# A one-column activation ahead of ScalarE's queue, and two weight splits placed behind exponentials, in an attention and feed-forward kernel

## The chip, the core and the metric

The kernel runs on one core of a Trainium2 chip. A core has TensorE (PE, matrix products into PSUM banks), VectorE (DVE), ScalarE (ACT), GpSimd (POOL) and SyncE (SP), which issues most of the transfers. The metric is the device time of one execution in microseconds (us), the median of several runs.

## What is computed

Four batches of eight heads with 576 positions of 64 values pass through attention with random features, then through two feed-forward blocks:

```python
q_p, k_p = phi(q * s), phi(k * s)   # phi(x) = exp(proj - sq - max) / sqrt(m), proj = x @ omega.T
num, den = q_p @ (k_p.T @ v), q_p @ sum(k_p)
x = num / den                        # 2304 tokens x 512
x = ((x @ w_a) * (x @ w_b)) @ w_out  # 1536 hidden
out = relu(x @ w_in2) ** 2 @ w_out2  # 2048 hidden
```

The weights of the feed-forward blocks arrive as 64-bit numbers, whose two 32-bit words the kernel itself turns into a pair of fp32r values (a high and a low part).

## The kernel before

**The stages.** First a prologue (`prologue`, L233) makes an identity matrix, transposes omega on TensorE into PSUM (L245), and copies it in three forms on ScalarE (OMS L247, OMZ L250, twice, and OM L251). Then lanes of attention work run, written as generators. `k_steps` (L407) handles a pair of k heads: it loads k and v (L310, L410), transposes k in four products (`t1_main`, L324; the product is L330, the copy from PSUM is S, L333), projects onto omega (`phi_wide`, L278: product L285, minimum over features on VectorE L289, exponentials on ScalarE L291, one for each head and slab), and multiplies the features with v (L423). `kt_steps` does the same for the last 64 positions of two pairs (the "tail": transpose L273, copy T L275, `phi_wide`, product L396). `q_steps` transposes and projects q, and forms the quotient that becomes a stretch of `x_all`. The lanes of the first batch stand at the beginning (`start_lanes`, L805): the first k pair alone, then q pairs and k pairs by turns. After them come passes over blocks of 256 tokens and weight columns `f` (`a_units`, products L610 and L635), with the rest of the attention lanes woven in, and at the end the second feed-forward block.

**The weights.** `load` (L125) fetches one or two 512 KB pieces into a `raw` buffer, of which there are two. `split` (L142) turns them into the high and low parts: on ScalarE L151, L152 and L163, on VectorE L155, L159, L164, L168 and L172. `load_split` (L184) issues the loads at once, and puts the split on a list with a count of steps; `step()` counts down and `split_next` runs the split when the count is zero, at the latest when the weights are needed. `get_w(f)` asks for w_a and w_b of column block f with a count of 3, `get_wo(n)` for w_out's rows. The first of them are asked for between the steps of the first lanes: `get_w(0)` after the lanes' second step, `get_wo(0)` after the eighteenth.

**What sets the order.** The code's order is only the first word. A planner that knows the dependencies, but estimates durations and transfers, puts the instructions of each engine into a fixed order when the program is built; what it takes to be ready first goes first, and the engine's queue then waits for its instructions one after the other. PSUM banks are handed out in turn by `at_bank` (L228), eight of them, so that the first q pair's transposes take the bank of omega's transpose. Loads on SP stand in one queue: omega, k, v, w_a, w_b, q, the next k, w_out and so on.

Of the kernel before, what the change touches and what calls it, by code (L numbers as in the profile page):

```python
# [8 lines left out]
F32 = mybir.dt.float32  # L9
# [4 lines left out]
ACTF = mybir.ActivationFunctionType  # L14
# [21 lines left out]
def f32(ap):  # L36
    return ap.bitcast(F32)


def i32(ap):  # L40
    return ap.bitcast(I32)
# [3 lines left out]
def kernel(  # L45
# [13 lines left out]
    nc = tc.nc  # L59
# [18 lines left out]
    wpool = ctx.enter_context(tc.tile_pool(name="wpool", bufs=FA))  # L78
# [46 lines left out]
    def load(*parts):  # L125


        raw = top["raw"].tile([128, 2, 512, 2], I32, tag="raw", name="raw")
        for x, (w, f, rows) in enumerate(parts):
            t = raw[:, x]  # L130
            if rows:
                nc.sync.dma_start(
                    out=t.rearrange("p f w -> p (f w)"), in_=w[f * 128:(f + 1) * 128, :]
                )
            else:
                nc.sync.dma_start(
                    out=t.rearrange("p (k f) w -> p k (f w)", k=KC),
                    in_=w[:, f * 256:(f + 1) * 256].rearrange("(k p) f -> p k f", p=128),
                )
        return raw[:, 0:len(parts)]  # L140

    def split(raw, t):  # L142

        n = raw.shape[1]
        up = raw[:, :, :, 1]
        u = raw[:, :, :, 0]
        a = top["cut"].tile([128, 2, 512], F32, tag="a", name="a")[:, 0:n]
        p = top["cut"].tile([128, 2, 512], F32, tag="p", name="p")[:, 0:n]  # L150
        nc.scalar.activation(out=a, in_=f32(up), func=ACTF.Copy, scale=WORD_SCALE)  # L151
        nc.scalar.activation(  # L152
            out=u, in_=raw.bitcast(U16)[:, :, :, 1], func=ACTF.Copy, scale=2.0 ** 7,
        )
        nc.vector.tensor_scalar(  # L155
            out=i32(p), in0=i32(a), scalar1=3, scalar2=0x7FFFF000,
            op0=ALU.logical_shift_left, op1=ALU.bitwise_and,
        )
        nc.vector.scalar_tensor_tensor(  # L159
            out=i32(p), in0=i32(a), scalar=-0x80000000, in1=i32(p),  # L160
            op0=ALU.bitwise_and, op1=ALU.bitwise_or,
        )
        nc.scalar.copy(out=t[:, :, 0, :], in_=p)  # L163
        nc.vector.scalar_tensor_tensor(  # L164
            out=u.bitcast(U32), in0=up.bitcast(U32), scalar=23, in1=u.bitcast(U32),
            op0=ALU.logical_shift_left, op1=ALU.bitwise_or,
        )
        nc.vector.tensor_scalar(  # L168
            out=i32(a), in0=i32(p), scalar1=-0x00800000, scalar2=None,
            op0=ALU.bitwise_and,  # L170
        )
        nc.vector.scalar_tensor_tensor(  # L172
            out=t[:, :, 1, :], in0=u.bitcast(U32), scalar=2.0 ** -43, in1=a,
            op0=ALU.mult, op1=ALU.mult,
        )
# [4 lines left out]
    def split_next():  # L180
        _, _, fn = waiting.pop(0)
        fn()

    def load_split(key, parts, t, steps, then=None):  # L184
        while len(waiting) > 1:
            split_next()
        raw = load(*parts)

        def fn():
            split(raw, t)  # L190
            if then:
                then()

        waiting.append([steps, key, fn])
# [11 lines left out]
    def get_pair(key, steps, pool, tag, *parts):  # L206
        t = pool.tile([128, 2, 2, 512], F32R, tag=tag, name=tag)
        load_split(key, parts, t, steps)
        return t[:, 0], t[:, 1]
# [4 lines left out]
    ap2 = actx.enter_context(tc.tile_pool(name="ap2", bufs=2))  # L214
# [11 lines left out]
    state = {"at": [0, 1, 2, 3, 4, 5, 6, 7], "n": 0}  # L226

    def at_bank(shape, name):  # L228
        i = state["at"][state["n"] % len(state["at"])]
        state["n"] += 1  # L230
        return bank(i, shape, name)

    def prologue():  # L233
        make_identity(nc, ident)
        nc.sync.dma_start(out=om[:, 0, :], in_=omega)
        nc.sync.dma_start(out=om[:, 1, :], in_=omega)


        nc.vector.memset(V, 1.0)
        nc.vector.memset(VT, 1.0)  # L240
        nc.vector.memset(VT[64:128, :, :, 0, :], 0.0)
        nc.vector.memset(VT[0:64, :, :, 1, :], 0.0)
        nc.vector.memset(OMZ, 0.0)
        ps = at_bank([128, M], "ps_om")
        nc.tensor.transpose(ps, om.rearrange("p a d -> p (a d)"), ident)  # L245

        nc.scalar.mul(out=OMS, in_=ps, mul=-SCALE)  # L247
        for x in range(2):
            r = slice(64 * x, 64 * x + 64)
            nc.scalar.mul(out=OMZ[r, x, :], in_=ps[r], mul=-SCALE)  # L250
        nc.scalar.copy(out=OM[:, 0, :], in_=OMS)  # L251
        nc.vector.tensor_tensor(out=OM[:, 1, :], in0=OMS, in1=f32(OM[:, 0, :]), op=ALU.subtract)
# [25 lines left out]
    def phi_wide(rows, dst):  # L278


        n = 2 * len(rows)
        nm = ap2.tile([128, n], F32, tag="nm", name="nm", bufs=4)
        ps = at_bank([128, n, M], "ps_p")
        for x, s in enumerate(rows):
            nc.tensor.matmul(  # L285
                ps[:, 2 * x:2 * x + 2].rearrange("p h m -> p (h m)"), lhsT=s,
                rhs=OMZ.rearrange("p h m -> p (h m)"), start=True, stop=True,
            )
        nc.vector.tensor_reduce(out=nm, in_=ps, axis=AXX, op=ALU.min)  # L289
        for x in range(n):  # L290
            nc.scalar.activation(  # L291
                out=dst[:, x, :], in_=ps[:, x, :], func=ACTF.Exp, scale=-1.0,
                bias=nm[:, x:x + 1],
            )

    class Side:
# [41 lines left out]
        def proj(self, slabs, dst):  # L338

            oo = [i * 128 for i in slabs]
            if self.wide:
                phi_wide([self.s[:, o:o + 128] for o in oo], dst)
                yield
                return
            for n, o in enumerate(oo):
                nm = ap2.tile([128, 2], F32, tag="nm", name="nm", bufs=4)
                ps = at_bank([128, 2, 2, M], "ps_p")
                for x in range(2):  # L350
                    nc.tensor.matmul(  # L351
                        ps[:, x].rearrange("p a m -> p (a m)"), lhsT=self.s[:, x, o:o + 128],
                        rhs=OM.rearrange("p a m -> p (a m)"), start=True, stop=True,
                    )
                c = ap2.tile([128, 2, M], F32, tag="c", name="c", bufs=2)
                nc.scalar.copy(out=c, in_=ps[:, :, 1, :])  # L356
                for x in range(2):
                    nc.vector.tensor_tensor_reduce(  # L358
                        out=c[:, x, :], in0=ps[:, x, 0, :], in1=c[:, x, :], scale=1.0,
                        scalar=3.0e38, op0=ALU.add, op1=ALU.min, accum_out=nm[:, x:x + 1],  # L360
                    )
                for x in range(2):
                    nc.scalar.activation(
                        out=dst[:, 2 * n + x, :], in_=c[:, x, :], func=ACTF.Exp, scale=-1.0,
                        bias=nm[:, x:x + 1],
                    )
                yield
# [5 lines left out]
    def kt_steps(b, g):  # L373
# [13 lines left out]
        yield  # L387
        kp = ap2.tile([128, 2, M], F32, tag="qp", name="kpt", bufs=2)
        phi_wide([st], kp)
        yield  # L390

# [123 lines left out]
    def qt_steps(b, g):  # L515
# [4 lines left out]
        yield  # L520
        qp = ap2.tile([128, 2, M], F32, tag="qp", name="qp", bufs=2)
        phi_wide([st], qp)
        yield
        ps = at_bank([128, 2, 128], "ps_qt")
# [70 lines left out]
    wa, wb, wo = {}, {}, {}  # L595
# [205 lines left out]


    prologue()

    def start_lanes():  # L805
# [23 lines left out]


    def get_w(f):
        wa[f], wb[f] = get_pair(("a", f), 3, wpool, "w", (w_a, f, False), (w_b, f, False))

    wo_order = [(pi, f) for pi, x in enumerate(PASSES) for f in range(x[1], x[2])]
    wo_made = set()
# [37 lines left out]
    def get_first():  # L873
        for f in range(W_FIRST):
            get_w(f)
            yield
            yield
            get_wo(f)
            yield
        for f in range(W_FIRST, 3):  # L880
            get_wo(f)
            yield
# [112 lines left out]
```

## Time and profile before

| | us |
|---|---|
| median of 3 runs | 1050.73 |
| lowest and highest of them | 1049.35, 1052.2 |
| the profiled execution, its own time | 1052.61 |
| span of the profiled execution | 1050.8 |

The span runs from the first to the last instruction that the profile holds; the execution's own time has 1.81 us around it. All times below are counted from the span's start. In rows of the timeline the columns are the start, the time from the first to the last of the instructions merged in the row, the engine, the line, the operation, the tile written and those read, the shape and the count; in brackets stands how long the engine had waited and what ended the wait.

### The profile page before, as it was taken

Reading aid. Unit: us, or ns where it says so; the run is one execution under the profiler, and the core shown is the slowest. Engines: PE = TensorE matmul, PEld = TensorE weight load, DVE = VectorE, ACT = ScalarE, POOL = GpSimd, SP = SyncE. Lnnn points to the kernel's source line nnn. Section 1 sums busy time; section 2 is a strip of 40 time slices with the busy share of each in tenths; the row PEclk is TensorE's granted clock in tenths of the full one; section 3 lists DMA queues with packets and bytes.
Section 4 is the critical chain, followed back from the end, with each engine's and each line's share of the span. In section 5 each row is a group of like instructions: output and inputs, shape, how many; then the busy total and the mean of one; then the engine's idle time right before and its main releaser. Section 6 shows DMA issues by size and latency. Waiting matters only on the chain.

```text
span 1050.8 us, 14948 instructions
## 1 busy us (share of the span) xinstructions
PE 1024.0 (97%) x5641; PEld 873.6 (83%) x5641; DVE 526.8 (50%) x1274; ACT 471.2 (45%) x1079; POOL 28.9 (3%) x54
## 2 busy tenths in 40 slices
PE   4899999999999999999999999999999999999998
PEld 3789989999988877788888888788788888888887
DVE  4788885665654445444337987722222322322222
ACT  4887757554455443333326665522322322322232
POOL 3100101000000000000000000000000000000000
PEclk9999999999999999999999999999999999999999
DMA  6846864663432211312227664300200200100010
GB/s 166 242 148 205 267 233 120 210 209 95 142 105 80 63 46 56 95 62 70 66 87 264 230 220 174 107 1 0 81 1 1 71 1 1 51 1 1 0 41 21
DMA packets 83144, 105.90 MB, mean 101 GB/s; under 512 B 26240, under 2 KB 65152, under 8 KB 83072
## 3 DMA queue, kind: packets, MB, share of 16 engines
q1 hardware_dynamic: 81536, 103.37, 30.7%
q0 software_dynamic: 1536, 1.58, 0.5%
q8 instruction: 45, 0.74, 0.3%
q14 instruction: 27, 0.22, 0.1%
HBM read 87.62 MB, written 17.30 MB: 100 GB/s over the span
## 4 chain that ended last, share of the span: by engine, by line
PE 88%; DVE 4%; DMA 3%; ACT 3%; issue 1%; SPq 1%; ACTq 0%; DVEq 0%
PE abw L610 19%; PE o L764 19%; PE ph L777 18%; PE y L635 12%; PE ab L610 7%; PE ps_n L481 3%; PE ps_p L285 2%; PE ps_kv L423 2%; PE ps_p L351 2%; PE ps_qt L474 1%; DMA raw<-in_moe_w_out_dram 1%; PE ps_t L330 1%; DMA qn<-in_q_dram 1%; DVE p L159 1%; PE ps_x L492 1%
## 5 line engine op out<-in xcount | busy, mean ns | idle before, releaser
L635 PE MATMUL y<-gs,wo 128*128 128x256 f32 (+1 forms) x864 | 177.2, 345 | 0.0
L764 PE MATMUL o<-w,ss 128*128 128x512 f32 x702 | 170.9, 390 | 1.4 <-ACT ss L786 1.4
L777 PE MATMUL ph<-yx,w 128*128 128x512 f32 (+1 forms) x780 | 169.8, 368 | 0.0
L777 PEld LDWEIGHTS ph<-yx,w 128*128 128x128 f32 x780 | 137.4, 188 | 25.3
L785 DVE TENSOR_TENSOR r<-r 128x512 f32<-128x512 f32 (+1 forms) x80 | 51.1, 639 | 209.8 <-ACT r L784 209.8
L764 PEld LDWEIGHTS o<-w,ss 128*128 128x128 f32 x702 | 130.5, 188 | 29.7 <-ACT ss L786 2.2
L635 PEld LDWEIGHTS y<-gs,wo 128*128 128x128 f32 x864 | 136.6, 190 | 15.2
L610 PE MATMUL abw<-x_all,w 128*128 128x512 f32 x576 | 146.6, 398 | 0.0
L784 ACT ACTIVATE r<-ph 128x512 f32<-128x512 f32 (+1 forms) x80 | 44.5, 556 | 208.4 <-PE ph L777 208.2
L610 PE MATMUL ab<-x_all,w 128*128 128x256 f32 x864 | 132.9, 295 | 0.3 <-DVE x_all L549 0.2
L610 PEld LDWEIGHTS abw<-x_all,w 128*128 128x128 f32 x576 | 105.5, 189 | 19.2
L610 PEld LDWEIGHTS ab<-x_all,w 128*128 128x128 f32 x864 | 115.0, 193 | 1.5 <-DVE x_all L549 0.5
L787 DVE TENSOR_TENSOR ss<-r,ss 128x512 fp32r<-128x512 f32 (+1 forms) x80 | 51.1, 639 | 46.6 <-ACT ss L786 40.0
L610 PE MATMUL abw<-x_mid,w 128*128 128x512 f32 x288 | 73.1, 400 | 0.0
L786 ACT CAST ss<-r 128x512 fp32r<-128x512 f32 (+1 forms) x80 | 46.2, 577 | 51.5 <-DVE r L785 51.5
L610 PEld LDWEIGHTS abw<-x_mid,w 128*128 128x128 f32 x288 | 52.1, 189 | 9.8
L358 DVE CUSTOM_DVE_ANT_0 c<-ps_p,c 128x128 f32<-128x128 f32 x152 | 37.8, 287 | 32.5 <-ACT c L356 32.0
L701 ACT CAST gs<-a_s 128x256 fp32r<-128x256 f32 (+1 forms) x96 | 40.6, 433 | 28.3 <-DVE a_s L700 28.1
L164 DVE SCALAR_TENSOR_TENSOR raw<-raw 128x1024 uint32<-128x1024 uint32 (+1 forms) x40 | 42.5, 1062 | 13.4 <-ACT raw L152 13.3
L152 ACT ACTIVATE raw<-raw 128x1024 int32<-128x1024 uint16 (+1 forms) x40 | 40.8, 1020 | 11.4 <-DMA raw<-in_moe_w_out_dram 9.3
L702 DVE TENSOR_TENSOR gs<-a_s,gs 128x256 fp32r<-128x256 f32 (+1 forms) x96 | 42.8, 454 | 5.3 <-ACT gs L701 4.2
L151 ACT ACTIVATE a<-raw 128x1024 f32<-128x1024 f32 (+1 forms) x40 | 40.6, 1014 | 10.9 <-DMA raw<-in_moe_w_out_dram 5.6
(109 smaller groups left out, 1212.9 us busy)
## 6 DMA issues: line engine op xcount, KB each, us to landing
wo<-wo_d SPq DMA_DIRECT2D x60, 512.0 KB, 3.5
raw<-in_moe_w_out_dram SPq DMA_DIRECT2D x28, 512.0 KB, 4.8
raw<-in_moe_w_in_dram SPq DMA_DIRECT2D x16, 512.0 KB, 3.9
raw<-in_moe_w_a_dram SPq DMA_DIRECT2D x12, 512.0 KB, 4.8
raw<-in_moe_w_b_dram SPq DMA_DIRECT2D x12, 512.0 KB, 6.1
wo_d<-wo SPq DMA_DIRECT2D x12, 512.0 KB, 3.4
kn<-in_k_dram SPq DMA_DIRECT2D x16, 256.0 KB, 3.5
V<-in_v_dram SPq DMA_DIRECT2D x16, 256.0 KB, 3.4
```

The source lines that it names most:

```text
L151: nc.scalar.activation(out=a, in_=f32(up), func=ACTF.Copy, scale=WORD_SCALE)
L152: nc.scalar.activation(out=u, in_=raw.bitcast(U16)[:, :, :, 1], func=ACTF.Copy, scale=2.0 ** 7,)
L164: nc.vector.scalar_tensor_tensor(out=u.bitcast(U32), in0=up.bitcast(U32), scalar=23, in1=u.bitcast(U32), op0=ALU.logical_shift_left, op1=A ...
L610: nc.tensor.matmul(ps, lhsT=wv[:, s_, kc, :], rhs=x[..., kc, m_, :], start=(kc == 0 and (s_, m_) == TERMS[0]), stop=(kc == KC - 1 and (s_, ...
L635: nc.tensor.matmul(y_part(pi, f, c), lhsT=wo[pi, f][:, s_, c * 128:(c + 1) * 128], rhs=g[:, m_, :],  start=(f == f0 and (wide or c % 2 == ...
L702: nc.vector.tensor_tensor(out=g[:, 1, c], in0=a_s, in1=f32(g[:, 0, c]), op=ALU.subtract)
L764: nc.tensor.matmul(op[t], lhsT=s_t[f][:, s_, t * 128:(t + 1) * 128], rhs=wo2[f][:, m_, :], start=(f == 0 and (s_, m_) == TERMS[0]), stop=( ...
L777: nc.tensor.matmul(ps, lhsT=wv[:, s_, kc, :], rhs=y[:, kc, m_, :], start=(kc == 0 and (s_, m_) == TERMS[0]), stop=(kc == KC - 1 and (s_, m ...
L784: nc.scalar.activation(out=r, in_=ps, func=ACTF.Relu, scale=1.0 / W_SCALE)
L785: nc.vector.tensor_tensor(out=r, in0=r, in1=r, op=ALU.mult)
L786: nc.scalar.copy(out=s_t[f][:, 0, :], in_=r)
L787: nc.vector.tensor_tensor(out=s_t[f][:, 1, :], in0=r, in1=f32(s_t[f][:, 0, :]), op=ALU.subtract)
```

## The change

```diff
@@ in load_split
         def fn():
-            split(raw, t)
+            if key in (("a", 0), ("o", 0)):
+                with tc.issue_after(state["exp"].ins):
+                    split(raw, t)
+            else:
+                split(raw, t)
             if then:
                 then()
@@ in prologue
     def prologue():
+        warm = ap2.tile([128, 1], F32, tag="den", name="warm", bufs=3)
+        nc.vector.memset(warm, 0.0)
+        nc.scalar.activation(out=warm, in_=warm, func=ACTF.Exp)
         make_identity(nc, ident)
@@ in phi_wide
         for x in range(n):
-            nc.scalar.activation(
+            state["exp"] = nc.scalar.activation(
                 out=dst[:, x, :], in_=ps[:, x, :], func=ACTF.Exp, scale=-1.0,
                 bias=nm[:, x:x + 1],
             )
@@ in get_w
-        wa[f], wb[f] = get_pair(("a", f), 3, wpool, "w", (w_a, f, False), (w_b, f, False))
+        wa[f], wb[f] = get_pair(("a", f), 3 if f else 7, wpool, "w", (w_a, f, False), (w_b, f, False))
```

The prologue gets a memset of one column on VectorE and an exponential of that column on ScalarE, both ahead of everything else in the code. `phi_wide` keeps its last exponential in `state["exp"]`. The split of the first w_a and w_b has a count of 7 instead of 3, so that it stands in the code behind the first k pair's step with the products with v, and not behind its first projections. `tc.issue_after` lays down that what the split issues on ScalarE comes behind the kept exponential in ScalarE's order; it is an order of issue, not a wait for a result, and other engines are not bound by it. When the split of w_a and w_b is written, the kept exponential is the second one of the first tail (`kpt`). When the split of the first w_out is written, after the lanes' twenty-first step, it is the last one of the second k pair. The loads stand where they stood, and no other operation is added or taken away.

## Rows read from the trace of the kernel before

**Rows 1.** Stretches: length, busy us and count by engine, PEclk, DMA share, GB/s.

```profile
13.14:20.00 6.86, 4.84 (x12) 3.59 (x13) 4.86 (x7) 6.62 (x15) 0.00 (x0) 1.00 0.34 99
20.00:60.00 40.00, 35.66 (x243) 30.71 (x242) 32.23 (x62) 35.32 (x98) 4.72 (x8) 1.00 0.72 218
60.00:150.00 90.00, 89.32 (x684) 84.46 (x684) 77.13 (x166) 64.80 (x154) 9.41 (x16) 1.00 0.67 212
```

The engines stand in the order PE, PEld, DVE, ACT, POOL.

**Rows 2.** Timeline of ScalarE from 0 to 23 us.

```profile
11.85 1.28 ACT L151 ACT_TABLE_LOAD   x1 [11.85 <-DMA raw<-in_moe_w_b_dram]
13.14 1.12 ACT L151 ACTIVATE a<-raw 128x1024 f32<-128x1024 f32 x1
14.16 0.27 ACT L247 ACTIVATE OMS<-ps_om 128x128 f32<-128x128 f32 x1
14.32 0.54 ACT L250 ACTIVATE OMZ<-ps_om 64x128 f32<-64x128 f32 x2
14.88 0.30 ACT L251 CAST OM<-OMS 128x128 fp32r<-128x128 f32 x1
15.21 0.59 ACT L333 COPY S<-ps_t 128x512 f32<-128x512 f32 x1
15.69 0.27 ACT L275 COPY T<-ps_tt 128x128 f32<-128x128 f32 x1
...
17.82 0.38 ACT L333 COPY S<-ps_t 128x256 f32<-128x256 f32 x1
...
18.68 1.14 ACT L291 ACTIVATE kp<-ps_p,nm 128x128 f32<-128x128 f32 x4
...
22.77 0.66 ACT L291 ACTIVATE kpt<-ps_p,nm 128x128 f32<-128x128 f32 x2
```

**Rows 3.** Timeline of TensorE's matmuls from 0 to 30 us.

```profile
3.22 0.45 PE L245 MATMUL ps_om<-ident,om 128*128 128x128 f32 x1 [3.22 <-DMA om<-in_omega_dram]
...
4.90 1.11 PE L330 MATMUL ps_t<-ident,kn 128*128 128x128 f32 x4 [1.24 <-DMA kn<-in_k_dram]
...
5.80 0.42 PE L273 MATMUL ps_tt<-ident,kt 128*128 128x128 f32 x1
...
14.91 0.69 PE L330 MATMUL ps_t<-ident,qn 128*128 128x128 f32 x2 [8.69 <-ACT OMZ L250]
...
15.85 3.78 PE L285 MATMUL ps_p<-OMZ,S 128*128 128x256 f32 x8 [0.24 <-ACT S L333]
...
19.42 0.77 PE L285 MATMUL ps_p<-OMZ,T 128*128 128x256 f32 x2
...
24.15 0.61 PE L396 MATMUL ps_kt<-VT,kpt 128*128 128x130 f32 x4
...
28.12 1.95 PE L423 MATMUL ps_kv<-V,kp 128*128 128x65 f32 x16
```

**Rows 4.** Timeline: the smallest memset, one on VectorE; waits: SP's for VectorE.

```profile
0.24 0.10 POOL L976 MEMSET const-float32-0.0<- 128x1 f32 x1 [0.24 <-issue]
...
1.96 0.27 DVE L243 MEMSET OMZ<- 128x256 f32 x1
...
SPq L410 <- DVE OMZ L243: 0.2, 1, 0.2
```

The last row's columns are the wait in total, the number of waits and the longest, in us.

**Rows 5.** Timeline of SP, and issues from 4.0 to 4.6: KB, us to landing.

```profile
4.27 0.50 SPq L310 DMA_DIRECT2D qn<-in_q_dram  x1
...
qn<-in_q_dram SPq DMA_DIRECT2D x1, 128.0 KB, 8.7
```

**Rows 6.** Timeline of VectorE: the first minimum over the projections.

```profile
17.95 0.69 DVE L289 TENSOR_REDUCE nm<-ps_p 128x4 f32<-128x512 f32 x1 [0.58 <-PE ps_p L285]
```

**Rows 7.** Timeline of SP: the first reload of a raw buffer.

```profile
21.57 0.37 SPq L136 DMA_DIRECT2D raw<-in_moe_w_a_dram  x1
```

**Rows 8.** Timeline: the fourth split of w_a and w_b ends; line L610 to 70 us.

```profile
67.20 1.23 DVE L172 SCALAR_TENSOR_TENSOR w<-raw,a 128x1024 fp32r<-128x1024 uint32 x1
...
L610 PE MATMUL ab<-x_all,w x72: 278/283/472, 46.5 to 69.8; 128*128 128x256 f32 x72
```

In the last row the times are the shortest, middle and longest in ns, then the first and last start in us.

## The prediction

> **What bounds the kernel now.** I read the table of stretches first, to see where TensorE is not supplied, and then the opening of each engine's queue, to see why. From 60 to 150 us the PE column is 89.32 of 90, but from 13.14 to 20 us it is 4.84 of 6.86, and in the 40 us that follow PE and ScalarE stand almost level, 35.66 and 35.32 of 40 [rows 1]. So the opening is short of work, the stretch to 60 us is limited by PE and ScalarE together, and from there on PE alone counts. A microsecond that PE gains in the opening lasts to the end only if ScalarE can follow until 60 us.
>
> ScalarE's own queue shows why the opening is empty. It does nothing for 11.85 us: its first instruction is the activation table's load and behind it L151, the first operation of the split of w_a and w_b, and that waits for w_b's transfer. L247, which needs only the transposed omega, stands behind it and starts at 14.16 [rows 2]. That transpose was finished at 3.67, the first k pair's four transposes at 6.01 and the tail's at 6.22. Then PE stops for 8.69 us at the transposes of the first q pair, which write a PSUM bank that L250 still has to read, and the k projections (L285) come behind them at 15.85 [rows 3].
>
> **The change part by part.** *The memset and the one-column activation.* The memset stands first on VectorE, ahead of V's memset. Its price is bounded by the 0.10 us of a 128x1 memset on GpSimd and the 0.27 us of the 128x256 one on VectorE, and SP waits 0.2 us for VectorE's memsets ahead of its load of V already [rows 4]. I take 0.1 us, by the one that has its size; it delays every transfer that SP issues from V on, so it is a real cost: +0.1, at most +0.3. The activation itself is bounded by nothing and by the 0.27 us of L247, and the table load takes 1.28 us [rows 2]; started near 1.1 us, both end by 2.7. They lie under the wait for the transposed omega, which ends at 3.67 [rows 3]; if omega came before that they would cost what they stick out.
>
> *The prologue's and the first k pair's copies move up.* With L151 gone from the head of ScalarE's queue, L247, L250, L251, L333 and L275 run when their PSUM tiles are ready, from 3.7 to about 7 us instead of from 14.16. That takes 0.27 + 0.54 + 0.30 + 0.59 + 0.27 = 1.97 us of work out of the stretch after 13.14 us, besides the 1.28 us of the table load before it [rows 2].
>
> *What is late next.* PE's queue is the point on which everything turns. Its next instructions are not the k projections but the two transposes of q. Their transfer is issued at 4.27 us, behind w_a and w_b on SP, and lands 8.7 us after its issue, at 12.97 us [rows 5]. Nothing in the change touches SP's order. So the wait of 8.69 us for L250 turns into one of some 6.8 us for q. Will the new order on PE still put q first? The order is fixed when the program is planned. That L151 was placed ahead of L247 tells that the plan takes the weights to be there before omega is transposed; q's load is the very next issue after w_b's, so the plan must take q to be there about then as well. The k projections need L251 and L333 after L250, 0.30 + 0.59 us more, and in that gap the q transposes are ready and PE is free. I therefore expect the same PE order as now.
>
> Then PE gets its q at 12.97 + 0.1, transposes until 13.7 (0.69 us, [rows 3]) and starts the k projections at 13.7 instead of 15.85: 2.15 us earlier. The eight passes and the tail's two take 4.34 us now (15.85 to 20.19, [rows 3]) and the same then, until 18.1.
>
> *The exponentials and the split.* The first minimum starts 2.10 us after the projections and takes 0.69 [rows 6]; so the first four exponentials run at about 16.5, the next four follow the eighth pass (17.5, then a minimum) at 18.2 and the tail's two end at about 20.0. Their work, with the second four like the first, is 2 x 1.14 + 0.66 = 2.94 us [rows 2]. The split of w_a and w_b is pinned behind the tail's, so L151 starts at 20.0 instead of 13.14: 6.9 us later, and with it the reuse of its raw buffer, whose next load was issued at 21.57 [rows 7].
>
> *ScalarE's account.* Between 13.14 and 20 it is busy for 6.62 us now [rows 1]. Then it has only q's copy, 0.38 [rows 2], and the 2.94 us of exponentials: 3.32. It does 3.30 us less in this stretch and has 1.97 us done beforehand, so at 20 us it is 1.3 us behind, while PE is 2.15 us ahead. VectorE has the same split still before it. w_out's split, pinned behind the second k pair's exponentials, moves work that fills gaps now into the stretch where ScalarE is nearly full; its amount is the same.
>
> *The sum.* If PE decides the stretch to 60 us: -2.15 + 0.1 = -2.05. If ScalarE decides: +1.3 + 0.1 = +1.4. As the two are level there but PE alone counts from 60 us on, I weigh PE's end twice: (2 x -2.05 + 1.4) / 3 = -0.9 us. The profiled execution took 1052.61 us, a span of 1050.8 and 1.81 around it; it lies 1.88 above the median of the three runs, 1050.73. Against its own time the forecast is 1051.7, against the median **1049.8**.
>
> **The rivals.** *A: the k projections get through.* If the plan puts the first k pair's projections ahead of the q transposes, they start when L333 is done, near 6.7 us, and end 4.34 us later at 11.0; with a minimum and two exponentials the pair's last ends near 12.4, before w_b has landed at all. The split is then not delayed, 1.97 + 2.94 = 4.9 us of ScalarE's work leave the full stretch, and PE is ahead by its 4.34 us and by the first pair's products with V and its tail's, 1.95 us (as the second pair's sixteen) and 0.61 [rows 3]: 6.9 in all. Between 4.9 and 6.9 I take 5.9: 1044.8. Against it speaks the order argument above; for it, that the order of the changed program is not in this trace and a little shift in the plan is enough. The same time would follow if PE could let a ready product overtake a waiting one. The Trainium skill, "TensorE: Matmul & The Clock Gate", section "Step-by-step: what each phase is for", says that only weight loads are pulled ahead and matmuls stay in program order; no row here shows it either way, and by it the q transposes do hold the projections up, if they stand first.
>
> *B: slower, through the weights.* All later splits pass through the same two raw buffers and the same two engines. If the 6.9 us by which the first split is late are handed on, the first matmuls to suffer are those of the fourth pair of weights: its split ends at 68.43, and the 72 matmuls that the first three pairs hold (2 products of 4 chunks and 3 terms each) are issued by 69.8 [rows 8]. That leaves 1.4 us of slack, so up to 5.5 us are exposed. The gaps that VectorE has from 20 to 60 (32.23 of 40) and ScalarE's (35.32 of 40) [rows 1] take part of it back; I price it at 4, giving 1054.7. It decides from the point at which that split ends after the fourth pair's first matmul could start. For it: ScalarE and PE are both near full until 60 us. Against it: between 20 and 60 us VectorE and ScalarE together have over 12 us free, ten times the 1.3 us that ScalarE lacks.
>
> *C: the change does not do what it says.* The pin could be without effect if the planned order had the split behind the exponentials anyway; rows 2 show the opposite, so this gets nothing.
>
> **How the numbers follow.** The q wait with its -0.9 has 0.65, A 0.21, B 0.14. A change in so early an order can also displace later waits by a microsecond or two, so I give the likeliest case -4 to +2 around the bounds -2.05 and +1.4, that is 1046.7 to 1052.7. The range reaches down to A with its larger gain, 1043.8, and up into B to 1053.5. A measurement of this kernel can tell about 0.3%, 3.2 us, from no change. A is faster by more than that. Of the likeliest case I put 0.15 below -3.2 and 0.03 above +3.2, nearly all the rest lies within. B is slower in four of five cases. Faster: 0.21 + 0.15 = 0.36; slower: 0.03 + 0.11 = 0.14; within: 0.50.
>
> **What would show it.** In the changed kernel's trace the table load starts near 1 us and L247 near 3.7. Right is: the q transposes on PE wait for q's transfer, end near 13.7, and L285 starts there; the tail's exponentials end near 20 and L151 follows. Wrong, by A, is L285 near 6.7, with L151 near 13. Wrong by B is PE idle between 65 and 95 us before weights (L610) whose split ended late. A new wait on the raw buffer's reload on SP that is over 7 us later than 21.57 would point the same way.

## The result and the profile after

The changed kernel takes 1056.69 us (median of 6 runs, 1055.34 to 1061.2), the kernel before on the same chip 1051.49 (6 runs, 1049.35 to 1052.27): a ratio of 1.0058, 95% interval 1.0039 to 1.0077, some 6 us slower. The forecast was 1049.8 in 1043.8 to 1053.5. The profiled execution took 1056.12 us, with a span of 1054.3: 3.5 us more than the span before. It lies a little below its kernel's median, as the one before lay above its own, so the profile shows 3.5 of the some 5 to 6 us.

Behind the prologue the changed kernel's lines stand 7 further down (L285 is L292, L291 L298, L330 L337, L333 L340, L610 L617); `load` and `split` keep theirs. First the table of stretches, as in [rows 1]:

```profile
13.14:20.00 6.86, 6.86 (x33) 5.90 (x32) 1.81 (x3) 3.10 (x12) 0.00 (x0) 1.00 0.30 82
20.00:60.00 40.00, 32.41 (x202) 27.20 (x202) 30.96 (x60) 34.15 (x88) 5.05 (x8) 0.96 0.68 208
60.00:150.00 90.00, 87.58 (x675) 83.06 (x674) 75.12 (x159) 64.98 (x156) 9.42 (x16) 1.00 0.63 197
```

Up to 20 us the change does what it says: from 13.14 us on PE is busy all the time. Then it is worse off than before twice: 32.41 us of work against 35.66 from 20 to 60, with the granted clock at 0.96, and 87.58 against 89.32 from 60 to 150.

ScalarE's timeline after, beside [rows 2]:

```profile
0.74 1.28 ACT L240 ACT_TABLE_LOAD   x1 [0.74 <-PEq L983]
2.03 0.20 ACT L240 ACTIVATE warm<-warm 128x1 f32<-128x1 f32 x1
3.54 0.28 ACT L254 ACTIVATE OMS<-ps_om 128x128 f32<-128x128 f32 x1 [1.30 <-PE ps_om L252]
...
5.91 0.59 ACT L340 COPY S<-ps_t 128x512 f32<-128x512 f32 x1 [1.34 <-PE ps_t L337]
...
15.37 1.14 ACT L298 ACTIVATE kp<-ps_p,nm 128x128 f32<-128x128 f32 x4 [1.31 <-DVE nm L296]
17.07 1.14 ACT L298 ACTIVATE kp<-ps_p,nm 128x128 f32<-128x128 f32 x4 [0.56 <-DVE nm L296]
18.09 0.65 ACT L298 ACTIVATE kpt<-ps_p,nm 128x128 f32<-128x128 f32 x2
19.97 0.27 ACT L437 COPY kvr<-ps_kv 128x130 f32<-128x130 f32 x1 [1.23 <-PE ps_kv L430]
20.13 1.14 ACT L151 ACTIVATE a<-raw 128x1024 f32<-128x1024 f32 x1
21.17 1.14 ACT L152 ACTIVATE raw<-raw 128x1024 int32<-128x1024 uint16 x1
22.18 0.28 ACT L410 COPY kvt<-ps_kt 128x130 f32<-128x130 f32 x1
22.33 0.62 ACT L340 COPY S<-ps_t 128x512 f32<-128x512 f32 x1
```

And TensorE's matmuls, beside [rows 3]:

```profile
12.02 0.66 PE L337 MATMUL ps_t<-ident,qn 128*128 128x128 f32 x2 [6.15 <-DMA qn<-in_q_dram]
12.47 1.06 PE L292 MATMUL ps_p<-OMZ,S 128*128 128x256 f32 x2
...
18.38 0.28 PE L337 MATMUL ps_t<-ident,kn 128*128 128x128 f32 x1
...
18.67 0.65 PE L292 MATMUL ps_p<-OMZ,S 128*128 128x256 f32 x2
...
23.00 1.13 PE L292 MATMUL ps_p<-OMZ,S 128*128 128x256 f32 x4 [2.14 <-ACT S L340]
...
24.19 1.03 PE L292 MATMUL ps_p<-OMZ,S 128*128 128x256 f32 x4
...
31.63 1.10 PE L481 MATMUL ps_qt<-ident,qp 128*128 128x128 f32 x4 [1.18 <-ACT qp L298]
33.40 1.13 PE L292 MATMUL ps_p<-OMZ,S 128*128 128x256 f32 x4 [0.67 <-ACT S L340]
...
39.97 1.21 PE L430 MATMUL ps_kv<-V,kp 128*128 128x65 f32 x8 [1.27 <-ACT kp L298]
...
43.23 1.91 PE L292 MATMUL ps_p<-OMZ,S 128*128 128x256 f32 x4
```

The second k pair's transposes were done on PE at 18.66, so that their copy out of PSUM (S, L340) had its input by 19. In ScalarE's queue it stands behind a copy that waits for PE until 19.97 (L437), and then behind L151 and L152 of the moved split; it runs at 22.33, and PE's next projections wait for it, 2.14 us. In e12 below, where that split is left out, the same copy runs at 20.40, so the split's share of the delay is 1.9 us. All of PE's waits from 20 to 46 us end with ScalarE: the four above, 0.46 at 26.11 and 0.20 at 42.21 make 5.92 us. Before, the same stretch had four, 1.83 us in all. Soon after the one at 39.97 the clock falls: the four projections at 43.23 take 1.91 us where those at 24.19 took 1.03. The same stretches of both kernels, the one after first:

```profile
20.00:46.00 26.00, 20.09 (x120) 16.82 (x120) 21.76 (x39) 22.70 (x57) 5.05 (x8) 0.93 0.61 181
41.00:46.00 5.00, 4.80 (x23) 3.95 (x23) 3.98 (x9) 4.09 (x13) 1.17 (x2) 0.66 0.78 223
84.00:110.00 26.00, 24.19 (x181) 22.21 (x181) 22.01 (x54) 17.39 (x42) 3.13 (x6) 1.00 0.58 185
```

```profile
20.00:46.00 26.00, 24.06 (x167) 20.87 (x166) 21.62 (x44) 23.23 (x69) 4.72 (x8) 1.00 0.66 197
41.00:46.00 5.00, 4.78 (x36) 4.36 (x36) 4.31 (x11) 5.00 (x18) 1.17 (x2) 1.00 0.63 193
84.00:110.00 26.00, 25.82 (x193) 23.98 (x192) 22.99 (x54) 19.85 (x47) 4.70 (x8) 1.00 0.69 222
```

A clock of 0.66 of 2.4 GHz over 41 to 46 means about two thirds of that time at the lower level, 1.2 GHz: some 5 x 0.34 = 1.7 us of work not done. This is one execution. All six of the changed kernel have a granted clock of 0.994 to 0.997 over the whole, while of the 94 executions of the kernel before that ran beside the experiments 91 have 0.998 to 1.000. (1 - clock) times the length is 4.8 us in the mean for the changed kernel and 1.0 us for the kernel before. By this estimate nearly 4 of the 6 us are time at the lower clock, more than the profiled execution shows. With 5.92 - 1.83 = 4.1 us of waits that is 5.8 us, and PE goes from 3.4 us ahead at 20 us to 2.8 behind at 46, a loss of 6.2 in this execution. The table of PE's progress shows this for all kernels:

```
us by which PE has done the same matmul work later (+) or earlier (-)
than in the kernel before, at its times (us)
                            20    46    60    84   110   145   160  1000
the change                -3.4  +2.8  +1.8  +1.6  +4.0  +4.2  +3.6  +3.5
e1 activation alone       -1.5  -1.6  -1.7  -1.6  -0.5  +0.5  +1.0  +1.4
e2 two pins alone         -3.2  +4.2  +3.1  +3.1  +5.1  +5.2  +3.1  +2.6
e3 without second pin     -3.0  +0.9  +0.2  +0.7  +4.1  +5.1  +4.5  +4.8
e4 without first pin      -1.4  -0.6  -3.2  -1.6  -1.6  -2.4  -5.5  -7.5
e5 behind the copy        -2.4  +2.5  +2.3  +2.1  +4.1  +4.5  +2.4  +1.5
e6 q ahead of weights     -8.8  +1.8  +1.4  +6.4 +11.1 +11.5 +10.9 +11.2
e10 short splits, changed -2.0  +3.2  +2.0  +2.3  +3.2  +4.7  +0.8  -2.0
e11 short splits, before  -0.9  -1.1  -2.4  -1.8  -0.4  +1.6  -2.3  -3.1
e12 first split out       -2.5  -2.3  -3.9  -0.2  +4.7  +4.6  +4.0  +2.7
e13 second pin by itself  -1.2  +0.0  -2.6  -2.0  -2.2  -2.6  -5.7  -7.1
e14 first weights again   -2.7  +6.3  +5.2  +5.0  +5.8  +6.1  +7.4  +5.6
e15 pin half way          -2.1  +3.2  +0.9  +0.7  +3.2  +3.1  +0.0  -0.9
e16 e12 and e14 together  -2.5  -0.7  -2.4  -1.8  +0.7  +2.2  -0.2  +0.4
e17 e14's edit on before  -0.6  -0.7  -0.4  -0.4  -0.2  +0.7  +1.0  +1.0
```

It is worked out from the traces: each matmul counts with the lower quartile of the distances between starts in its line before, and for each kernel the time is read at which the sum is the same. It is of one execution each, while the ratios below are of several. It tells where time is lost, by stretch, but not to the microsecond: up to 93 us e14 has the same instructions in the same order as the change on PE, ScalarE and VectorE, and is at +6.3 where the change is at +2.8; e12 and e16 have one order up to 68 us, and are 1.6 us apart at 46. In its profiled execution the changed kernel loses from 20 to 46 us and again from 84 to 110.

The second loss has its sign on SP, whose timeline around the reload for the sixth pair of weights is, after and then before:

```profile
84.09 0.61 SPq L417 DMA_DIRECT2D V<-in_v_dram  x1
84.89 0.56 SPq L136 DMA_DIRECT2D raw<-in_moe_w_a_dram  x1
```

```profile
77.03 0.37 SPq L136 DMA_DIRECT2D raw<-in_moe_w_a_dram  x1
...
82.62 0.61 SPq L410 DMA_DIRECT2D V<-in_v_dram  x1
```

The reload that stood at 21.57 [rows 7] is issued at 26.41, 4.8 us later. By the reload for the fourth pair the delay is down to 3.1 us (53.47 against 50.41), and then it grows to 7.9 us here. So most of it arises between 50 and 77 us; e12 below shows that it arises without a late first split too. The last step (L172) of the sixth pair's split runs at 98.83, 8.2 us later than the 90.59 of the kernel before. The reload's raw buffer came free late, at 83.34, when the fifth pair's L172 ended (77.0 before); and on SP it now also stands behind a load of V that waits for its own buffer until 84.09.

### The profile page after: what moved, and what is told of

It reads as the page before. It is cut to its first block, busy times and chain, and to the rows that moved or that the text cites. A ratio compares the mean times of both kernels' runs of the same rounds, so it can differ in the third digit from the quotient of the medians.

```text
span 1054.3 us, 14946 instructions
## 1 busy us (share of the span) xinstructions
PE 1025.2 (97%) x5641; PEld 875.5 (83%) x5641; DVE 527.4 (50%) x1275; ACT 473.1 (45%) x1080; POOL 29.3 (3%) x54
## 4 chain that ended last, share of the span: by engine, by line
PE 87%; DMA 4%; DVE 4%; ACT 4%; issue 1%; SPq 0%; ACTq 0%; DVEq 0%
PE o L771 19%; PE abw L617 19%; PE ph L784 18%; PE y L642 12%; PE ab L617 7%; PE ps_n L488 2%; PE ps_p L292 2%; PE ps_p L358 2%; PE ps_kv L430 2%; DMA raw<-in_moe_w_out_dram 2%; PE ps_qt L481 1%; DMA raw<-in_moe_w_b_dram 1%; PE ps_t L337 1%; DMA qn<-in_q_dram 1%; ACT raw L152 1%
## 5 line engine op out<-in xcount | busy, mean ns | idle before, releaser
L617 PE MATMUL abw<-x_all,w 128*128 128x512 f32 x576 | 146.6, 398 | 0.0
L617 PE MATMUL ab<-x_all,w 128*128 128x256 f32 x864 | 131.8, 295 | 1.4 <-ACT x_all L505 0.7
L617 PEld LDWEIGHTS abw<-x_all,w 128*128 128x128 f32 x576 | 105.4, 189 | 19.3
L617 PEld LDWEIGHTS ab<-x_all,w 128*128 128x128 f32 x864 | 114.8, 193 | 2.8 <-ACT x_all L505 0.9
L617 PE MATMUL abw<-x_mid,w 128*128 128x512 f32 x288 | 73.0, 399 | 0.0
L617 PEld LDWEIGHTS abw<-x_mid,w 128*128 128x128 f32 x288 | 52.1, 189 | 9.7
L164 DVE SCALAR_TENSOR_TENSOR raw<-raw 128x1024 uint32<-128x1024 uint32 (+1 forms) x40 | 42.5, 1063 | 11.9 <-ACT raw L152 11.8
L152 ACT ACTIVATE raw<-raw 128x1024 int32<-128x1024 uint16 (+1 forms) x40 | 40.5, 1012 | 11.9 <-DMA raw<-in_moe_w_out_dram 9.4
L151 ACT ACTIVATE a<-raw 128x1024 f32<-128x1024 f32 (+1 forms) x40 | 40.6, 1014 | 10.5 <-DMA raw<-in_moe_w_out_dram 6.6
```

Source lines behind the costliest of these rows:

```text
L152: nc.scalar.activation(out=u, in_=raw.bitcast(U16)[:, :, :, 1], func=ACTF.Copy, scale=2.0 ** 7,)
L164: nc.vector.scalar_tensor_tensor(out=u.bitcast(U32), in0=up.bitcast(U32), scalar=23, in1=u.bitcast(U32), op0=ALU.logical_shift_left, op1=A ...
L617: nc.tensor.matmul(ps, lhsT=wv[:, s_, kc, :], rhs=x[..., kc, m_, :], start=(kc == 0 and (s_, m_) == TERMS[0]), stop=(kc == KC - 1 and (s_, ...
```

## The experiments

Ratios are to the kernel before on the same chip, with the 95% interval.

### Which part of the change costs: e1 to e4

e1 leaves both pins out, and the count at 3:

```diff
-                with tc.issue_after(state["exp"].ins):
-                    split(raw, t)
+                split(raw, t)
-        ... get_pair(("a", f), 3 if f else 7, ...
+        ... get_pair(("a", f), 3, ...
```

> ScalarE's-queue theory (the pinned split stands ahead of the second k pair's copy from PSUM, PE starves behind it between 20 and 45 us): nothing is pinned here, L151 heads ScalarE's queue again and waits for w_b until about 11.8 us; only the table load's 1.28 us are taken out from behind that wait, so L247 starts near 13 instead of 14.2 and the time is 1050 to 1051.5. Weights theory (the late split makes all later weights late): the same, as the split is as early as before. If the one-column activation itself cost the time, it would be 1056 or more.

Measured: 0.9995 [0.9985, 1.0005]. The activation alone keeps the order of before, and its gain of 1.5 to 1.7 us stands until 84 us; by 145 it is gone. So even in this kernel's own order a gain in the opening did not last to the end.

e2 leaves out the three lines of `warm`:

> ScalarE's-queue theory: the pins alone make the loss, 1055 to 1058; the first k projections start near 12.5 us as in the changed kernel and PE waits about 2 us for the second k pair's copy near 23. Weights theory: also 1055 to 1058. If the loss needed the activation, it would be 1050 to 1052.

Measured: 1.0056 [1.0042, 1.0069], as the whole change. The loss comes from the pins.

e3 keeps the first pin alone, e4 the second (with the count of 3), both with the activation:

```diff
-            if key in (("a", 0), ("o", 0)):
+            if key == ("a", 0):          # e3;  e4: if key == ("o", 0)
```

> Both theories put the loss on the split of w_a and w_b that starts at 20 us instead of 13: 1055 to 1057, as the changed kernel. If w_out's pin carried the loss, it would be 1051 to 1053.

> Only w_out's split is pinned, and L151 of w_a and w_b heads ScalarE's queue again. If the first pin makes the loss: 1050 to 1052.5. Weights theory: w_out's first split ends some 3 us later and hands on at most that, 1051 to 1054. If w_out's pin carried the loss: 1055 to 1057.

Measured: e3 1.0034 [1.0020, 1.0048], e4 0.9940 [0.9925, 0.9955]. The loss needs the first pin, and without it the rest of the change beats both kernels, 1046.6 us. The parts do not add up: +3.6 us with the first pin, -6.3 with the second, and 6.1 slower with both. Beside the first pin, the second gains nothing. The gain of e4 has two places in the table, 2.6 us from 46 to 60 and 3.1 from 145 to 160. At the second the kernel before has this on PE and on VectorE:

```profile
152.10 0.33 PE L542 MATMUL ps_xt<-ident,xh 128*128 128x128 f32 x1 [1.47 <-DVE xh L459]
...
153.68 4.03 PE L610 MATMUL ab<-x_all,w 128*128 128x256 f32 x22 [0.17 <-DVE x_all L549]
```

```profile
149.58 1.23 DVE L159 SCALAR_TENSOR_TENSOR p<-a,p 128x1024 int32<-128x1024 int32 x1
150.84 0.16 DVE L458 RECIPROCAL den<-den 64x2 f32<-64x2 f32 x1
151.03 0.69 DVE L168 TENSOR_SCALAR a<-p 128x1024 int32<-128x1024 int32 x1
151.75 0.29 DVE L459 TENSOR_TENSOR xh<-ps_nt,den 64x128 f32<-64x128 f32 x1
```

Two steps of a split stand between the steps of the quotient for which PE waits, and behind the wait PE runs slowly: the granted clock is 0.67 from 153.68 to 157.71. This fall of the clock, some 1.7 us, is not in every execution of the kernel before; of the 26 that ran beside e4, 13 have a granted clock of 1.000 over the whole. So the trace shows more of the gain than the medians do. In e4 the quotient is done in time and the same 22 matmuls take 2.88 us:

```profile
149.35 2.88 PE L617 MATMUL ab<-x_all,w 128*128 128x256 f32 x22 [0.67 <-DVE x_all L556]
```

That the order comes out well there is not something the pin aims at; e13 below tries one small shift of it.

### Is it the copy that the split delays, or the split's amount: e5, e10, e11

e5 pins the first split behind the second k pair's copy and not the tail's exponentials:

```diff
-                with tc.issue_after(state["exp"].ins):
+                with tc.issue_after(state["exp" if key[0] == "o" else "copy"].ins):
-                nc.scalar.copy(out=self.s, in_=ps)
+                state["copy"] = nc.scalar.copy(out=self.s, in_=ps)
-        ... 3 if f else 7 ...
+        ... 3 if f else 12 ...
```

> The first split is pinned behind the second k pair's copy from PSUM instead of behind the tail's exponentials. ScalarE's-queue theory: that copy runs near 19 instead of 22.3 us, PE's wait of 2.1 us near 23 is gone and no half clock follows at 41 to 45; 2 to 4 us come back, 1052 to 1055. Weights theory: L151 starts at 20 or later, so every weight is as late as in the changed kernel and nothing comes back, 1056 to 1058.

Measured: 1.0040 [1.0027, 1.0053]. The copy now runs at 20.54, and the wait of 2.14 us is gone. PE is as late at 46 us all the same, +2.5, although its waits from 20 to 46 us come to 3.00 us only, the longest of them, 0.88 at 31.16, behind w_out's split: the granted clock of the stretch is 0.93, as in the changed kernel. With 1055.5 us some 1.9 of the 6 us come back, less than the first theory said and more than the second. So this one copy is not the whole of it.

e10 takes L159, L164 and L168 out of every split (VectorE's masks, so that the weights' parts are other values), e11 does it in the kernel before:

> The changed kernel with three of the five VectorE operations left out of every split (L159, L164, L168), so that the weights' low parts and signs are not formed; the loads, the ScalarE part and the order of the pins stay. Weights theory: the row of splits gets ahead again after the late start, PE finds its weights, and the time is within 2 us of the next run's, the kernel before with the same left out. ScalarE's-queue theory: the loss of 4 to 6 us between 20 and 45 us stands and the difference to the next run is as large as between the full kernels.

> The kernel before with the same three VectorE operations left out of every split, as the measure for the run ahead of it. PE is the limit from 60 us on, so it is only a little faster than the full kernel before: 1046 to 1051. Weights theory: it gains less by this than the changed kernel does, by 3 us or more. ScalarE's-queue theory: both gain the same within 2 us.

Measured: 0.9985 [0.9973, 0.9997] and 0.9972 [0.9959, 0.9986]: the two differ by 0.0013, 1.4 us, where the full kernels differ by 6.1. Up to 145 us, though, e10 is no earlier than the change: +3.2 against +2.8 at 46 us, +4.7 against +4.2 at 145. What it gains on the change lies behind that, 3.3 us from 145 to 160, where e11 gains 3.9 on the kernel before, and 2.7 us after 160. So VectorE's part of the splits is not what counts in the opening; ScalarE's, which e10 leaves whole, can be. Why the end comes out nearly level is not shown.

### The opening pushed further: e6

```diff
-    S0, SD = 1, 8
+    S0, SD = 12, 8
```

The first weights are asked for eleven steps later, so that q is loaded ahead of them and the k projections don't wait.

> The change with the first weights asked for only after the first q pair's and the second k pair's loads. ScalarE's-queue theory: q lands near 6 us, the first k projections start near 6.7, and the split comes behind the second k pair's work; PE is supplied 5 us earlier, 1046 to 1050. Weights theory: L151 starts near 20 and the next weights still later, 1056 to 1060.

Measured: 1.0086 [1.0071, 1.0102], the slowest of all, although PE is 8.8 us ahead at 20 us. It is slower than either theory said. The lead is gone at 46, at a granted clock of 0.74 from 20 to 46, and then PE waits openly for weights:

```profile
79.50 1.23 PE L617 MATMUL ab<-x_all,w 128*128 128x256 f32 x4 [2.71 <-ACT w L163]
```

### How much of the loss is the moved split's work: e12, e15

```diff
+            if key == ("a", 0):
+                nc.gpsimd.memset(f32(t), 0.0)
```

> Left out: the split of the first w_a and w_b; GpSimd writes zeros into their weight tiles instead. ScalarE loses some 3.3 us of work and VectorE some 5 us that the changed kernel has in front of them at 20 us. Theory (the moved split fills ScalarE's queue at 20 to 46 us ahead of what PE needs): PE, 3.4 us ahead of the kernel before at 20 us, is still at least 2.5 us ahead at 46 us, the wait of 2.14 us for the second k pair's copy is gone, and the time is 4 to 6 us under the changed kernel's, ratio to before 0.996 to 1.001. Rival (the loss comes from the order in which PE, ScalarE and VectorE pass the second and third pairs, whatever the split costs): PE is behind the kernel before at 46 us here too, and the time stays within 2 us of the changed kernel's, ratio 1.004 to 1.008.

Measured: 1.0020 [1.0005, 1.0034], 4.0 us under the changed kernel's: at the lower edge of the 4 to 6 us that the theory gave, and outside its range of ratios. In the opening the theory holds: PE's waits from 20 to 46 us are down to two, 1.77 us, the clock stays at 1.00, and the lead at 46 is 2.3 us, at 60 even 3.9. Then it loses 8.6 us from 60 to 110, at a clock of 0.97. In e12 the copy in the opening, then PE and ScalarE later:

```profile
20.40 0.59 ACT L342 COPY S<-ps_t 128x512 f32<-128x512 f32 x1
```

```profile
74.15 0.74 PE L619 MATMUL ab<-x_all,w 128*128 128x256 f32 x4 [2.75 <-ACT w L163]
```

```profile
72.06 1.10 ACT L152 ACTIVATE raw<-raw 128x1024 int32<-128x1024 uint16 x1 [2.85 <-DMA raw<-in_moe_w_b_dram]
```

A PE that is early meets weights that are late: the split waits for its transfer, and PE for the split. It is not the lateness of the first split that makes them late. In e12 that split's raw buffer is free at once, and SP reloads it 9.6 us earlier than in the kernel before; the reload for the sixth pair is 7.8 us late all the same:

```profile
11.93 0.37 SPq L136 DMA_DIRECT2D raw<-in_moe_w_a_dram  x1
...
84.85 0.55 SPq L136 DMA_DIRECT2D raw<-in_moe_w_a_dram  x1
```

The early reload gains nothing: its weights have landed at 19.58, and their split begins at 32.24, where it stands in ScalarE's order (30.72 before). What makes the later reloads late, from 50 us on, is not shown.

e15 pins the first split behind the first four exponentials (count 3 in place of 7):

> The changed kernel with the first split pinned behind the first four exponentials of the first k pair and not behind the last of its tail: L151 should run at about 16.5 us, half way between the 13 us of the kernel before and the 20.1 us of the changed one. Theory (the loss grows with how late the split comes into ScalarE's and VectorE's queues): PE loses half as much from 20 to 46 us, and the time lies between that of the run with the second pin alone (0.9940) and the changed kernel's (1.0058), at 0.998 to 1.003. Rival (any pin of the first split that parts it from the slack at 13 us costs the whole): 1.004 to 1.007. Second rival (the end is set by the order at 90 to 157 us, which falls one way or the other whatever the delay): outside both, under 0.997 or over 1.007.

Measured: 1.0007 [0.9993, 1.0020], inside the theory's range, for another reason than the theory's. L151 runs at 17.63. The opening loses nearly as much as with the full delay (5.3 us against 6.2; 2.1 ahead at 20, 3.2 behind at 46): the split's L163 now stands ahead of the second k pair's copy, and PE waits 2.31 us for that copy. What makes it better is above all the stretch from 145 to 160, where it gets back 3.1 us, some 1.7 of them because the clock does not fall there. So a loss in the opening that grows with the delay does not show: the first rival was right of the opening but not of the time, and the second names the stretch but missed with its range.

### The late weights: e14, e16, e17

```diff
-            proj(aps, wa[f], x)
+            proj(aps, wa[f if wide or not 2 < f < 6 else f - 3], x)
```

and the same for `wb`. The splits are all still made, but no matmul of the single row blocks waits for the late ones. e14 is the change with this edit, e16 is e12 with it, e17 the kernel before.

> Changed: in the passes of a single row block, the products for the fourth to sixth pairs of weights take the tiles of the first to third pairs, so that no matmul of 65 to 130 us has to wait for a late split; the splits are all still made. Theory (of the 4 us by which PE is late at 110 us, about 2 are lost from 90 to 110 us to splits that are 8 us late): PE is within 0.5 us at 110 us of where it is against the kernel before at 84 us, and the time is 1.5 to 2.5 us under the changed kernel's, ratio 1.003 to 1.0045. Rival (those 2 us go to copies and to VectorE's own queue, not to PE's wait for weights): the loss between 84 and 110 us is there all the same, ratio 1.005 to 1.007.

> Left out: the first split of w_a and w_b, whose weight tiles GpSimd fills with zeros. Changed: in the passes of a single row block the products for the fourth to sixth pairs of weights take the tiles of the first to third. Theory (two losses: the moved split in ScalarE's queue until 46 us, then PE waiting from 60 to 110 us for weights that are late): PE is 2 us or more ahead of the kernel before at 46 and 60 us and loses at most 1.5 us of that by 110 us; the time is 6 to 9 us under the changed kernel's, ratio to before 0.996 to 1.000. Rival (what is lost from 60 to 110 us is lost to copies and to VectorE's other work): PE is 3 to 5 us behind at 110 us, as without the split alone; ratio 1.001 to 1.004.

> The kernel before, changed in the same way: in the passes of a single row block the products for the fourth to sixth pairs take the tiles of the first to third. Theory: in the kernel before no split is late, PE is busy for 89.32 of the 90 us from 60 to 150, and the edit is worth nothing: 0.998 to 1.001. Rival (weights are short in both kernels, and the edit gains 2 us or more in either): 0.995 to 0.998.

Measured: e14 1.0056 [1.0036, 1.0076], e16 0.9984 [0.9970, 0.9997], e17 0.9993 [0.9981, 1.0005]. e14's time is what its rival said, yet from 84 to 110 us it loses 0.8, where the change loses 2.4: it comes out no better since its opening lost 9.0 us to 46 instead of 6.2. That is not the order, which is the change's on PE, ScalarE and VectorE up to 93 us, nor the waits, 5.76 us from 20 to 46, but the clock, 0.86 where the change has 0.93, and 0.90 against 1.00 up to 60. e14 and then the change:

```profile
20.00:46.00 26.00, 20.24 (x111) 16.88 (x111) 19.53 (x35) 20.17 (x50) 3.86 (x6) 0.86 0.51 146
46.00:60.00 14.00, 12.97 (x81) 11.14 (x81) 8.39 (x21) 10.46 (x29) 1.17 (x2) 0.90 0.77 237
```

```profile
46.00:60.00 14.00, 12.31 (x84) 10.38 (x83) 9.20 (x22) 11.46 (x32) 0.00 (x0) 1.00 0.80 258
```

So that the late weights cost the changed kernel anything in time is not shown: 1.0056 and 1.0058 are the same. They do cost e12, as e16 shows, whose opening keeps the clock at 1.00: at 100 us it is still 1.4 us ahead, from 60 to 110 it loses 3.1 us where e12 lost 8.6, and the time falls by 0.0036, 3.8 us, of which the granted clocks of the executions account for some 1.5 (0.995 to 1.000 in e12, 0.998 to 1.000 in e16). In the kernel before the same edit is worth 0.7 us, no more than its interval. Two figures of e16's expectation fail: it is 0.7 us ahead at 46 and not 2, and it loses 3.1 us by 110 and not 1.5. The waits that PE still shows there end with ScalarE's copies and VectorE's quotients, so the rival holds for that part.

### The gain by itself: e13

e4 without the one-column activation.

> The kernel before with w_out's first split alone pinned behind the exponentials, without the one-column activation. The run with both was at 0.9940. If the early table load gives its 1.5 us to the end there, this one is at 0.9950 to 0.9960. If the activation gives nothing in the end, as it gave nothing alone (0.9995), it is at 0.9935 to 0.9945. If the pair's gain was a chance of the planned order, which another small shift displaces, the gain is gone: 0.998 to 1.003.

Measured: 0.9949 [0.9932, 0.9966]. The gain of the second pin stands without the activation, in the same two places, and the activation adds 0.0009, 0.9 us, which the intervals cannot tell from nothing. So this one shift does not undo it, but why the planner's order is better at 50 and 150 us is not shown.

A third raw buffer, which would part the loads from the splits, was not tried.

## Why the prediction was wrong

**The prologue** was right. The table load starts at 0.74 and the omega copies at 3.54; PE, which stopped 8.69 us for L250 [rows 3], stops 6.15 for q. The memset of VectorE cost nothing that shows.

**The order on PE** was right in what counted. The transposes of q come first, the k projections follow at 12.47; only the tail's transposes, forecast where they were at 5.80, now come behind the first two of them, at 13.33; q came 1 us earlier than in [rows 5], so PE is 3.4 us ahead at 20 us instead of 2.15. Rival A, the projections ahead of q, is out: the first k pair's S was done at 6.5, and PE waited until 12.02 for q, with those projections behind it. That agrees with the Trainium skill, "TensorE: Matmul & The Clock Gate", section "Step-by-step: what each phase is for", by which matmuls keep their program order.

**The exponentials and L151.** L151 was forecast at 20.0 and measured at 20.13, but that is luck. The tail's exponentials ended at 18.74 and not at 20.0, and what then held L151 back is a copy that the forecast did not have: L437 stands ahead of it, and waited 1.23 us for PE, until 19.97.

**ScalarE's account and the sum** are the step that failed. The account was right in its figures (3.10 us of work from 13.14 to 20, 3.32 forecast), but it closed at 20 us, and the sum took a deficit of 1.3 us as the most that ScalarE could cost (+1.4 with the memset). What counts is not how much ScalarE has left but what stands ahead of what: the split, which ran under PE's wait and slow first projections, now stands between PE's transposes and PE's projections. PE waited 4.1 us more for ScalarE from 20 to 46 us, although ScalarE was not busier there (22.70 us against 23.23). The Trainium skill, "Perfetto Trace Analysis", section "Tensor Engine Instruction (MATMUL, LD_WEIGHTS)", says that ScalarE's and VectorE's queues are strictly first in, first out. The trace agrees: the second k pair's copy had its input at 18.66, and did not run in ScalarE's idle 1.23 us ahead of 19.97. The clock was in no term either, 1.7 us from 41 to 46 in this trace and by the estimate above nearly 4 of the 6 us in the mean of the executions. Forecast was -0.9 to the end; measured is a lead of 3.4 at 20 us that has turned into +2.8 at 46, and +3.5 at the end of the profiled execution.

**Rival B** named late weights, and in the changed kernel they are late: the reload for the sixth pair by 7.9 us, the end of its split by 8.2. But its mechanism, a first delay that is handed on, is not what the runs show: in e12 and e16 the first reload is 9.6 and 9.8 us early, and the sixth pair's 7.8 and 7.2 us late. Nor is its place right in the changed kernel: the fourth pair's split ends at 74.12 instead of 68.43, and PE has no wait above 0.15 us from 60 to 89 us. From 84 to 110 the changed kernel loses 2.4 us, of which e14 has 0.8 without the late weights; little of it is an open wait for L172 (0.21 us), and e1, which has no pin, loses 1.1 there. The wait for the fourth pair does come in e12 and e6 (2.75 and 2.71 us). The 4 us set for it are near the 3.8 that e16 gets back from e12, but by luck, since the change itself gets nothing back in e14. e12 makes the first 4.0 us and e16 the second 3.8; together they are more than the 6 us lost, for which the change's gain in the opening and the one split less of e12 are reasons that are argued, not shown.

**The change's gain** of 2 us and more in the opening did not last in e1, e6 and e12, and in e12 it went where PE had to wait for weights. A term for this, the time at which a pair's split ends against PE's need, was missing.

Left open: why the clock stays low longer in e14 than in the change, with the same order; what makes the reloads late from 50 us on; and how much of e4's gain at 46 to 60 us is the pin's own doing.

## What to carry to other kernels

Ask of a moved piece of work not how much it is, but which instruction it will stand in front of on an in-order queue, and who waits for that one; background work that fills a stall was free there, and here it cost PE 4.1 us of waits one stage later. Price the clock that falls behind such waits beside the waits themselves, and read the granted clock of every execution, not of the profiled one alone. Before calling late weights handed on, take the first delay away and see whether they are late still; here they were. Try each half of a change alone: here one half loses 3.6 us, the other gains 6.3, and both together lose 6.1.

## What the runs showed that was not expected

After gaps of PE that come to 5.92 us between 20 and 46, the granted clock went down to 0.66 from 41 to 46 while PE was busy for 4.80 of the 5 us: part of the price of the waits falls due behind them. The kernel before shows the same at 153.68, 4.03 us at a clock of 0.67 for 22 matmuls that take 2.88 in e4. Two kernels of one order can differ by 3.5 us through this, as e14 and the change do at 46 us.

Small changes in the first 20 us moved the end by -6.3 to +9.0 us, ratios 0.9940 to 1.0086, and the lead at 20 us does not tell the sign: the kernel with the largest lead, 8.8 us, is the slowest. Some 3 us of the gain of e4, e13 and e15 in their traces fall at 145 to 160 us, 1.7 of them a fall of the clock that they do not have; there the order of one split beside one quotient on VectorE is another than before.
